# Row loads turned on TensorE, one-operation piece transposes, a fifth summed step and a new instruction list in an H3 convolution and gMLP kernel

## The chip, the cores and the metric

The kernel runs on one core of a Trainium2 chip. A core has five engines that each run their own instruction stream and wait for each other through semaphores: TensorE (PE, matrix products, with the weight loads PEld beside them), VectorE (DVE), ScalarE (ACT), GpSimd (POOL) and SyncE (SP), which here only issues DMAs. The metric is device time in microseconds, lower is better. The kernel before takes 325.17 us (median of 9 runs, 324.26 to 326.95).

## The reference

The input is a sequence `A_q` of 2048 rows and 640 columns. A small vector `c` makes six modulation vectors from one weight, and two blocks follow, each with a layer norm in front and a gated residual behind:

```
sa, ca, ga, sb, cb, gb = silu(c) @ w_mod              # six vectors of 640
h  = layernorm(x) * (1 + ca) + sa
x  = x + ga * A(h, k, v)
h  = layernorm(x) * (1 + cb) + sb
x  = x + gb * B(h)

A: kv = shiftconv4(k, shift_k) * v                    # 4 taps along the sequence, per column
   y  = irfft(rfft(pad(kv)) * rfft(pad(ssm_k)))[:2048] + kv * ssm_D
   return h * y                                       # a long convolution, per column
B: z  = gelu(h @ w_in)                                # 640 -> 2 x 864
   z1, z2 = first half, layernorm(second half)
   return (z1 * (w_sp @ z2 + b_sp)) @ w_out           # w_sp mixes the 2048 rows
```

## The kernel before, in words

Block A works on five units of 128 columns. The long convolution is done as a Fourier transform by matrix products. For each unit there are two inputs, the filter (`XK`, with `ssm_D` added at its first sample, `add_D`, L390) and the product kv (`XU`). `stage1` (L400) multiplies them with a small table, `forward` (L427) with the table M2, in eight steps per unit. ACT keeps the filter's spectrum (`k_item`), and `u_item` (L446) multiplies it with the other one on DVE (`product`, four partial products). The inverse step comes in two forms. In a summed step the partial products are kept in float32 (tile `Tf`, two buffers), two half sums (`csum`, L466) on GpSimd or DVE make `W`, and TensorE does six matmuls. In an unsummed step TensorE takes all four partial products (tile `T`) with twelve matmuls and sums in PSUM. `SUMS` (L35) makes steps 1, 3, 5 and 7 summed ones. The result `Z` is turned, by DMA for units 0 to 3 (`last_stage`, tile `ZT`), on TensorE for unit 4 (`last_stage_pe`), and the last small product (`y`, `yl`) gives y, which is multiplied with the gated norm `gh` (`ym`, `yml`) and added to x (`resid`). `gh_mod` (L644) applies the modulation to `gh`, in products of 512 elements per partition on GpSimd or DVE (`ghm`).

The input kv comes first: k and v are read with transposing DMAs (`load_kv`, L502), four shifted products with diagonal matrices give the taps (`short_conv`, L519, with the diagonals from `sk`), DVE multiplies with v (L543), the result is written to a scratch tensor in DRAM (`kv_scr`) and read back in the layout of the transform.

Three small vectors are loaded at the start or early: `ssm_D` into every 16th partition of `D_col` (L736, after GpSimd has zeroed that tile, L269), `shift_k` into `sk_bf` (L737) and `c` into `c_bf` (L733), in each case with single values or groups of four spread over the partitions.

Block B begins with `z_group` (L838) for groups of four row blocks. The first group is turned on TensorE: it goes in two pieces of two row blocks, and `flip_piece` (L815) makes for each of the five column blocks one TensorE operation of two transposes into a PSUM tile with tag `sm` (two buffers) and one modulation on ACT or DVE. The other groups are turned by DMA. Then TensorE multiplies with `w_in` (tags `pu` and `pz`, two buffers each) and ACT applies gelu. After it the mixing loop (`mix`, `project`, L939 to L971) runs over the 16 row blocks.

All work up to the mixing loop is not run in the order in which it is written. Each piece is registered with `op(...)`, with the engines on which it may run, its inputs and outputs. `ORDER` (L40) is a list written out by hand that names every piece with its number and the engine (P, A, D, G, S) that runs it; `Plan.run` (L112) emits the pieces in this order. So each engine's order, and the order in SP's and ACT's DMA queues, is that of the list. Within it `fill` pieces (L910, sizes in `FILLS`, L34) are matmuls whose result nobody uses.

Of the kernel before, what the change touches and what calls it, by code (L numbers as in the profile page):

```python
# [33 lines left out]
FILLS = (4, 1, 4, )  # L34
SUMS = (1, 3, 5, 7)  # L35
# [5 lines left out]
A76 S3 D6 D94 D7 D12 D11 S4 A1 A9 D8 G95 D96 D115 S13 D103 D10 D116 A117 A118 D80 D5 P1019 P1020 P139 P142 A141 A140  # L41
A144 D17 P20 D97 S77 D98 A100 D143 P18 D81 D104 A105 P148 D109 A99 A106 D110 A111 S14 A112 P145 A150 S15 D21 D19 S16
P24 A26 D121 G101 D102 G119 D107 G108 S507 D120 G113 D25 P22 D23 P130 D511 D131 D132 A147 S28 A146 A149 P163 P153 A164
A154 G114 P136 A137 P151 A152 P127 G30 D128 G129 P159 A160 S82 D84 P155 A156 P219 P133 A134 G42 D512 D513 G135 P157
D514 S27 P161 A162 A158 A220 P35 S29 S78 D36 S79 P31 P167 D169 A168 P170 A171 S40 P33 D172 D32 P173 D34 A510 P176 D178
A174 P37 A175 A177 P165 D38 A166 P193 D194 P221 A222 P179 D180 S508 P45 A515 S39 P203 G195 G196 P223 P189 A224 G66
P181 D204 G205 G206 D190 A516 P209 D210 P225 S0 A2 P197 A198 D517 G138 A182 P213 D214 G215 A226 P47 S41 P183 D184 S83
D46 A518 P191 A192 P207 P199 D200 D48 D526 D527 P229 P243 A230 A244 P49 D50 S549 P239 A208 A240 P245 A246 P227 S509
D522 A228 P43 D44 D185 P233 G124 G125 A234 S85 D87 D519 S88 P249 A250 G186 D523 P237 A238 P231 A232 P550 P247 A248
G216 P217 D218 P241 A242 P235 A236 P291 A292 P255 D256 P552 A553 D524 P211 D212 S51 P251 D90 D252 S554 P293 A528 A294  # L50
G520 P187 P275 D276 A188 G257 G258 G277 P201 A551 A202 P297 A298 P281 D282 P253 A254 G278 P265 D266 P295 P261 A529
A296 D525 P259 D530 P279 A280 A260 P557 D558 P555 S86 P315 A316 P299 D521 D262 G267 G54 G268 S52 S53 A300 S559 A122
S583 P283 G531 A284 D533 D537 D538 S64 D539 P309 A310 D534 D535 D536 G654 P317 A318 P263 P57 P285 D532 A541 P319 A320
P305 A306 D556 G575 D58 D286 G287 D542 A543 D264 D545 P59 P269 P311 A312 P301 A546 D544 D579 A302 D60 P560 D547 D658
D561 P303 A304 D123 D548 P321 P55 A322 G581 G582 P307 A308 D288 P313 A314 D56 D580 P61 D62 P323 D324 P363 P562 G576
A540 G577 G578 G639 P333 A364 P289 D563 A270 P365 A366 P337 A290 D334 P325 P357 D338 P367 D358 P584 D585 A326 P271
D272 A368 P71 S65 D72 P369 A370 G339 G340 P586 D587 P347 D348 P341 A342 P273 A274 P375 A376 D596 P588 D589 G660 S63
S89 G359 P387 A388 G360 D597 G349 G350 P361 D362 P371 A372 P373 A374 D656 P389 G602 A390 P590 D591 P353 D354 P69 D70
P385 P391 D600 A392 A386 A564 P327 D328 D598 S91 G697 D93 P335 A336 D593 P351 G601 P383 A384 P343 P393 D635 G636 P67
A352 D344 D599 A394 P73 P377 P395 A378 D68 P435 A436 P355 A356 P399 D74 G691 D396 D603 P439 A440 D400 P425 G633 S604  # L60
P605 D606 P345 A346 D426 P441 A442 G329 G330 P607 D608 G637 G638 P381 A382 P331 P379 G401 G402 G640 A380 D695 G696
P609 D610 A332 P405 D406 S75 P437 A438 P415 P611 D612 G613 P397 D416 A126 P419 D420 S92 P459 A460 P427 A428 P453 A454
P465 A466 P565 P457 P429 G661 S641 D592 D615 D618 D616 D614 A398 G421 G422 A458 D430 G628 P461 P417 D418 A567 P443
P409 D410 A462 A566 D619 A444 P403 A404 P463 A464 G634 P642 D643 G659 P449 A450 P423 P447 A448 D622 G431 G432 D620
A424 P644 D645 P481 D482 P433 P467 D468 P407 A434 A408 S738 P451 A452 G411 G412 G483 G484 P646 D647 G657 P413 G623
P501 D502 P648 P491 P469 G655 A414 A470 P487 D492 G493 D488 G494 P568 P455 A456 D621 A569 P485 P445 D649 A486 G503
G504 P497 D498 A446 P489 A490 P471 D472 G693 P495 P477 D478 A496 P505 A506 P499 A500 G651 S662 P663 D664 P479 A480
S570 P665 D666 G473 G474 G698 P475 A476 D617 P667 D668 P705 G692 P703 A704 D706 P669 D670 P701 G650 D671 D672 P699
D700 A702 G676 D677 D673 P571 D674 A572 P707 P730 G653 D708 D709 D711 D710 D740 D739 D712 P723 D713 D714 P573 A574
P716 D724 G741 D742 S737 D743 A744 P1021 P745 D731 D746 D755 P747 A748 D675 D715 D756 P749 A750 P753 A754 P751 D752  # L70
D694 D717 P799 A800 D718 D679 P805 A806 P778 G757 P771 D758 D760 A759 P761 A779 A762 P765 D721 A766 D678 D720 A772
D722 D680 D824 D719 D821 D822 P774 P769 P781 A770 P763 D823 D595 A775 P767 A768 D631 D594 D625 D764 A782 G825 D826
D827 D830 A828 D829 S831 D725 D626 P803 D727 A804 D728 P813 A814 D726 D652 D681 D685 D684 P801 A802 P792 P795 A793
D773 D732 D736 A796 P785 D683 P809 A810 D889 D627 P811 P788 A786 A833 D682 D632 D835 D836 A832 A812 D834 D686 D690
D687 D733 D624 D688 D689 P807 A808 A789 P879 A880 P837 A838 P869 P877 A878 D888 D629 A870 P875 D729 D890 D887 A876
P854 G891 D892 D893 A896 D776 D777 D894 D895 A855 D856 D735 P844 A845 D846 P840 D794 A841 D842 P851 P847 A848 P865
A866 D955 A852 D953 D787 P871 D853 A872 D630 D849 D857 P861 A862 P858 S897 A901 D902 A898 P867 D734 D954 A859 D900
P873 A874 A868 D956 G957 D899 P937 P903 A904 A938 P924 P913 D797 D958 A959 A914 D798 D962 P920 D780 A921 D961 D960
D790 S963 A925 D915 P935 A936 D783 D784 P927 A928 D791 G815 D816 P910 A911 D912 D916 P939 A940 A819 D818 P941 A942
D965 P917 P931 D850 A966 D905 P906 A932 A918 D964 D967 D968 P986 P969 A907 A970 D860 D863 D864 D839 D843 A987 P1009  # L80
A1010 D988 P972 G881 D882 A973 P993 A994 D886 P945 A946 D908 D919 P976 D929 D926 D930 A977 D883 P983 D922 D820 A984
D909 D971 D923 D995 D978 D974 P990 D975 A991 D992 P1003 A1004 G947 D948 D949 A884 A817 D985 P933 A934 D885 P979 A980
P1005 A1006 P1001 A1002 P999 A1000 P1011 A1012 D981 D982 P1007 D996 D989 G1013 A950 D1014 D1016 D1018 P997 D1017 A998
D1015 A952 A1008 P943 A944 D951
# [39 lines left out]
def kernel(  # L124
# [37 lines left out]
    d_fft = A_ssm_D.rearrange("(c g) -> g c", g=8)  # L162
# [42 lines left out]
    with ExitStack() as actx:  # L205
# [9 lines left out]
        sk_bf = consta.tile([P, ND, 4], BF16)  # L215
        c_bf = consta.tile([P, ND], BF16)
# [25 lines left out]
        def copy(e, dst, src):  # L242
            (e.copy if e is nc.scalar else e.tensor_copy)(dst, src)  # L243
# [25 lines left out]
        nc.gpsimd.memset(D_col[:], 0.0)  # L269
# [176 lines left out]
        def u_item(u, st):  # L446
# [4 lines left out]

            summed = st in SUMS
            ttag = "Tf" if summed else "T"

            def product(e):
                T_ = new(T, ttag, [P, KP, 2, 2, DU], F32 if summed else BF16)
                e.tensor_tensor(T_[:], tl[pu][:, :, :, None, :].to_broadcast([P, KP, 2, 2, DU]),  # L457
                                tl[KH][:, :, None, :, :].to_broadcast([P, KP, 2, 2, DU]), op=ALU.mult)
            op("D", "prod", product, r=[pu, KH], w=[T], new=[(T, ttag)])
# [99 lines left out]
        def ln1(n):  # L559
# [24 lines left out]
            op("DA", "ln1", stats, r=xs, w=[("mv1", n), ("gh", (0, n // TB))], new=[(tile_, "st1")])  # L584
# [111 lines left out]
        def last_stage_pe(u):  # L696
# [19 lines left out]
            for g in range(NT // TB):  # L716
# [9 lines left out]
                for ns in pieces(g):  # L726
# [3 lines left out]
                    resid(u, g, ns)  # L730


        op("SA", "ldc", lambda e: e.dma_start(c_bf[:], c[0].rearrange("(t p) -> p t", p=P)), w=["c"])  # L733
        op("A", "silut", lambda e: e.activation(warm[:], warm[:], ACT.Silu), w=["silut"])
        op("A", "silu", lambda e: e.activation(sc[:], c_bf[:], ACT.Silu), r=["c", "silut"], w=["silu"])
        op("S", "ldD", lambda e: e.dma_start(D_col[0:P:16, :], d_fft), w=["D"])  # L736
        op("SA", "ldsk", lambda e: e.dma_start(sk_bf[:], A_shift_k.rearrange("(t p) j -> p t j", p=P)), w=["skb"])  # L737
        op("D", "skc", lambda e: e.tensor_copy(sk[:], sk_bf[:]), r=["skb"], w=["sk"])
        index_bits(0, 2)
        f1_table()  # L740
        index_bits(2, 6)
        identity()
        for dt in range(ND):
            load_kv(dt)
            short_conv(dt)
        for u in range(NU):
            d0, du = u * DU, DU
            load_X("XK%d" % u, ssm_fft, u)
            load_X("XU%d" % u, kv_fft, u, [("kvs", (u, h)) for h in range(2 if u == 0 else 1)])
            add_D(u)  # L750
        m2_base()
        for i in range(NKC // KCH):
            m2_chunk(i)
        e_table()
# [265 lines left out]
```

## Time and profile before

| what | value |
|---|---|
| median of 9 runs | 325.17 us |
| the profiled execution, its own time | 327.34 us |
| its span, first to last instruction | 325.5 us |
| PE busy, share | 310.4 us, 95% |
| DVE busy, share | 210.0 us, 65% |
| ACT busy, share | 148.1 us, 45% |
| POOL busy, share | 93.5 us, 29% |
| mean granted TensorE clock | 0.983 |
| first stage of X1U0 starts at | 26.08 us |
| first output step of unit 3 starts at | 122.77 us |
| first MLP matmul starts at | 137.19 us |
| mixing loop starts at | 197.69 us |

How to read it: a profile line gives an engine, the line of the code (often that of a helper, L240 for nearly all matmuls, so the tile names tell more), the operation, output tile and input tiles without buffer numbers, and the shapes. The span is cut into 40 equal slices; a digit is the busy share of an engine in tenths, and PEclk is the clock that TensorE was granted, in tenths of full speed. DVE, for instance, is at 9 of 10 in most slices up to 130 us and at 2 to 4 in the mixing loop. The shares of the whole span are an average over stages with different limits. Every duration comes from one profiled execution.

### The profile page before, as it was taken

Reading aid. Unit: us, or ns where it says so; the run is one execution under the profiler, and the core shown is the slowest. Engines: PE = TensorE matmul, PEld = TensorE weight load, DVE = VectorE, ACT = ScalarE, POOL = GpSimd, SP = SyncE. Lnnn points to the kernel's source line nnn. Section 1 sums busy time; section 2 is a strip of 40 time slices with the busy share of each in tenths; the row PEclk is TensorE's granted clock in tenths of the full one; section 3 lists DMA queues with packets and bytes.
Section 4 is the critical chain, followed back from the end, with each engine's and each line's share of the span. In section 5 each row is a group of like instructions: output and inputs, shape, how many; then the busy total and the mean of one; then the engine's idle time right before and its main releaser. Section 6 shows DMA issues by size and latency. Waiting matters only on the chain.

```text
span 325.5 us, 6384 instructions
## 1 busy us (share of the span) xinstructions
PE 310.4 (95%) x2581; PEld 207.0 (64%) x2589; DVE 210.0 (65%) x464; ACT 148.1 (45%) x255; POOL 93.5 (29%) x121
## 2 busy tenths in 40 slices
PE   5969999899999998899999999999999999999996
PEld 2556889778889896555555555555555555555554
DVE  8967999999999898789675773442332222223333
ACT  4747999897879755377668674000000000000001
POOL 2531724659799898210111120000000000000000
PEclk9979999999999999789999999999999999999999
DMA  6999998997687785004226990465665554422231
GB/s 126 205 258 278 217 293 208 226 244 187 116 236 145 243 179 192 2 1 81 41 42 107 185 250 3 94 132 104 144 137 120 135 114 114 113 50 48 48 50 60
DMA packets 128868, 44.99 MB, mean 138 GB/s; under 512 B 117992, under 2 KB 128072, under 8 KB 128840
## 3 DMA queue, kind: packets, MB, share of 16 engines
q1 hardware_dynamic: 125672, 41.74, 59.2%
q10 hardware_dynamic: 3168, 2.86, 2.7%
q8 instruction: 20, 0.33, 0.4%
q14 instruction: 8, 0.07, 0.1%
HBM read 16.11 MB, written 5.24 MB: 66 GB/s over the span
## 4 chain that ended last, share of the span: by engine, by line
PE 74%; DVE 10%; DMA 7%; SPq 4%; ACT 2%; issue 1%; POOL 0%; DVEq 0%; POOLq 0%; ACTq 0%
PE ps L944 29%; PE pu L240 15%; PE pz L240 13%; PE po L965 9%; DMA ZT<-Z 5%; PE sm L240 5%; SPq L511 3%; PE s L240 3%; DVE T L457 2%; DVE Tf L457 2%; DMA X<-in_A_ssm_k_dram 2%; DVE st L570 1%; DVE big L543 1%; DVE X L243 1%; ACT X L243 1%
## 5 line engine op out<-in xcount | busy, mean ns | idle before, releaser
L944 PE MATMUL ps<-X,wT 128*128 128x432 bf16 x512 | 95.7, 346 | 0.0
L944 PEld LDWEIGHTS <-wT 128*128 128x128 bf16 x512 | 50.1, 98 | 42.2
L957 ACT COPY uT<-pt 128x896 bf16<-128x896 bf16 x1 | 0.9, 906 | 119.1 <-PE pt L956 119.1
L240 PEld LDWEIGHTS <-Z 128*128 128x128 bf16 x320 | 31.7, 100 | 27.5 <-issue 1.6
L240 PE MATMUL pu<-X,M 128*128 128x128 bf16 (+1 forms) x480 | 46.9, 239 | 1.5 <-DVE T L457 0.9
L240 PEld LDWEIGHTS <-M 128*128 128x128 bf16 x480 | 37.7, 99 | 6.9 <-issue 1.6
L947 DVE SCALAR_TENSOR_TENSOR u<-ps,bcol,G 128x432 bf16<-128x432 f32 x18 | 12.0, 668 | 42.1 <-PE ps L944 42.1
L243 ACT CAST X<-s 128x1024 bf16<-128x1024 f32 x32 | 32.7, 1021 | 4.4 <-PE s L240 4.3
L240 PE MATMUL pu<-big,Z 128*128 128x432 bf16 x160 | 33.6, 353 | 0.0
L965 PE MATMUL po<-w_o,uT 128*128 128x320 bf16 (+2 forms) x231 | 33.2, 295 | 0.1
L240 PE MATMUL pz<-big,Z 128*128 128x432 bf16 x160 | 33.2, 351 | 0.0
L466 POOL TENSOR_TENSOR W<-Tf 128x256 bf16<-128x256 f32 x38 | 28.0, 756 | 15.6 <-DVE Tf L457 14.8
L947 DVE SCALAR_TENSOR_TENSOR u<-ps,bcol,M 128x432 bf16<-128x432 f32 x14 | 9.3, 667 | 30.2 <-PE ps L944 30.2
L965 PEld LDWEIGHTS <-uT 128*128 128x128 bf16 (+1 forms) x231 | 22.2, 98 | 9.9 <-issue 0.2
L240 PEld LDWEIGHTS <-G 128*128 128x128 bf16 x360 | 26.9, 98 | 1.8
L243 ACT CAST KH<-pu 128x512 bf16<-128x512 f32 x40 | 22.9, 595 | 6.7 <-PE pu L240 6.7
L457 DVE TENSOR_TENSOR Tf<-pu,KH 128x1024 f32<-128x1024 f32 x20 | 24.2, 1218 | 1.6 <-PE pu L240 1.1
L457 DVE TENSOR_TENSOR T<-pu,KH 128x1024 bf16<-128x1024 f32 x20 | 24.2, 1217 | 0.6 <-PE pu L240 0.5
L967 DVE TENSOR_TENSOR ot<-po,xt 128x320 bf16<-128x320 f32 (+1 forms) x33 | 15.9, 482 | 12.7 <-PE po L965 12.7
L243 ACT CAST Z<-pz 128x512 bf16<-128x512 f32 x35 | 20.3, 590 | 6.7 <-PE pz L240 6.5
L240 PEld LDWEIGHTS <-X 128*128 128x128 bf16 x288 | 18.2, 99 | 7.8 <-DVE X L396 4.6
L888 DVE BATCH_NORM_STATS2 stz<-X 128x6 f32<-128x432 bf16 x32 | 18.2, 591 | 7.1 <-ACT X L882 7.1
(143 smaller groups left out, 413.2 us busy)
## 6 DMA issues: line engine op xcount, KB each, us to landing
wm<-in_w_mod_dram SPq DMA_DIRECT2D x4, 800.0 KB, 6.1
out_dram<-ot SPq DMA_DIRECT2D x15, 160.0 KB, 2.4
big<-in_B_w_in_dram SPq DMA_DIRECT2D x2, 1080.0 KB, 8.3
X<-in_A_ssm_k_dram SPq DMA_DIRECT2D x4, 512.0 KB, 6.2
kv_scr<-big SPq DMA_DIRECT2D x4, 512.0 KB, 3.5
X<-kv_scr SPq DMA_DIRECT2D x4, 512.0 KB, 4.9
xt<-in_A_q_dram SPq DMA_DIRECT2D x3, 640.0 KB, 6.2
wm<-in_w_mod_dram ACTq DMA_DIRECT2D x2, 800.0 KB, 7.3
```

Source lines behind the costliest of these rows:

```text
L240: nc.tensor.matmul(o, lhsT=w, rhs=x, start=start, stop=stop)
L243: (e.copy if e is nc.scalar else e.tensor_copy)(dst, src)
L457: e.tensor_tensor(T_[:], tl[pu][:, :, :, None, :].to_broadcast([P, KP, 2, 2, DU]), tl[KH][:, :, None, :, :].to_broadcast([P, KP, 2, 2, DU] ...
L466: e.tensor_tensor(tl[W][:, :, o, :], T_[:, :, 0, o, :], T_[:, :, 1, 1 - o, :], op=ALU.add if o else ALU.subtract)
L511: e.dma_start_transpose(tl[name][:, o + h * m:o + (h + 1) * m], src[0, h * m:(h + 1) * m, dt * P:(dt + 1) * P])
L543: e.tensor_tensor(vsl, tl[ps][:], vsl, op=ALU.mult)
L570: e.bn_stats(out=st[:, a, :], in_=xt[:, n, a * HS:(a + 1) * HS])
L888: op("D", "stz", lambda e, i=i, n=n, fc=fc: e.bn_stats(out=stz[:, n, fc, :], in_=tl[z2][:, i, fc * FC:(fc + 1) * FC]), r=[(z2, (i, fc))], ...
L944: nc.tensor.matmul(ps[:, :FC], lhsT=wTs[t][:, s_, :], rhs=tl["z2_%d" % (s_ // TB)][:, s_ % TB, fc * FC:(fc + 1) * FC], start=(s_ == 0), st ...
L947: nc.vector.scalar_tensor_tensor(u[:, sl], ps[:, :FC], bcol[:, t:t + 1], z1[t][:, sl], op0=ALU.add, op1=ALU.mult)
L965: nc.tensor.matmul(ps[:, :hi - lo], lhsT=uTs[t][:fsz[ft], ft, :], rhs=w_o[:fsz[ft], ft, lo:hi], start=(ft == 0), stop=(ft == NFT - 1))
L967: nc.vector.tensor_tensor(ot[:, lo:hi], ps[:, :hi - lo], xt[:, t, lo:hi], op=ALU.add)
```

## The change

- The three small vectors are read as rows (`small_load`): `shift_k` as 5 rows of 128 x 4, `ssm_D` as 80 rows of 8, `c` as 5 rows of 128. DVE or GpSimd spreads the 80 x 8 values into a zeroed tile of 80 x 128 (`dwide`). TensorE turns each with small matmuls against the identity (`small_turn`), and DVE or ACT copies the result out of PSUM.
- `MODE` replaces `SUMS`: steps 0, 2, 4, 5 and 7 are summed, five of eight. (A third mode is written in the code and not used.)
- `flip_piece` makes one TensorE operation of all ten transposes of a piece, into one PSUM tile with tag `s1` (one buffer); the five modulations follow.
- Row statistics (`ln1`) are bound to an engine by row block.
- `FILLS` has five entries (17 matmuls) instead of three (9). In the new list ten of them stand in front of the first transform and seven ahead of the first piece's transposes.
- `ORDER` is new throughout: other orders on every engine, other choices of engine. Half sums on GpSimd 38 to 43 and on DVE 2 to 7; row statistics on ACT 5 to 8 and on DVE 11 to 8; `ghm` on GpSimd 27 to 29; residuals on GpSimd 7 to 9; the loads of w_mod and q that stood on ACT's queue are on SP's; the first diagonal is made on ACT; the early gelu of the table load (L758) stands at the end of the list.

The numbers of the pieces shift, so the two lists can't be compared line by line; the list is cut here.

```diff
-FILLS = (4, 1, 4, )
-SUMS = (1, 3, 5, 7)
+FILLS = (4, 5, 1, 4, 3, )
+MODE = ('susussus', 'susussus', 'susussus', 'susussus', 'susussus')
 ORDER = """
-A76 S3 D6 D94 D7 D12 D11 S4 A1 A9 D8 G95 D96 D115 S13 D103 D10 D116 A117 A118 D80 D5 P1019 P1020 P139 P142 A141 A140
...
+D0 D100 D13 D14 A1 D15 G5 A2 A82 G101 D102 D103 S19 S21 D115 D116 A4 A16 D17 D6 D104 P1027 P7 A10 A23 P1028 P8 S83 A11
...
-            summed = st in SUMS
-            ttag = "Tf" if summed else "T"
+            mode = MODE[u][st]
+            summed = mode == "s"
...
-            op("DA", "ln1", stats, r=xs, w=[("mv1", n), ("gh", (0, n // TB))], new=[(tile_, "st1")])
+            op("D" if n % 8 < 4 else "DA" if n % 8 == 4 else "A", "ln1", stats, r=xs, w=[("mv1", n), ("gh", (0, n // TB))], new=[(tile_, "st1")])
...
-        nc.gpsimd.memset(D_col[:], 0.0)
...
-        op("SA", "ldc", lambda e: e.dma_start(c_bf[:], c[0].rearrange("(t p) -> p t", p=P)), w=["c"])
+        def small_load(name, shape, src):
+            op("SA", "ld1", lambda e: e.dma_start(new(name, "KH", shape)[:], src), w=[name], new=[(name, "KH")])
+
+        def small_turn(name, r, fn):
+            def turn(e):
+                fn(new(name, "sm", [P, 512], F32))
+            op("P", "turn1", turn, r=r + ["ident"], w=[name], new=[(name, "sm")])
+        small_load("skr", [ND, P, 4], A_shift_k.rearrange("(t p) j -> t p j", p=P))
+        small_load("Dr", [D // 8, 8], A_ssm_D.rearrange("(c g) -> c g", g=8))
+        small_load("cr", [ND, P], c[0].rearrange("(t p) -> t p", p=P))
...
-        op("S", "ldD", lambda e: e.dma_start(D_col[0:P:16, :], d_fft), w=["D"])
-        op("SA", "ldsk", lambda e: e.dma_start(sk_bf[:], A_shift_k.rearrange("(t p) j -> p t j", p=P)), w=["skb"])
-        op("D", "skc", lambda e: e.tensor_copy(sk[:], sk_bf[:]), r=["skb"], w=["sk"])
+        op("G", "dzero", lambda e: e.memset(new("Dw", "KH", [D // 8, P])[:], 0.0), w=["Dw"], new=[("Dw", "KH")])
+        op("DG", "dwide", lambda e: e.tensor_copy(tl["Dw"][:, 0:P:16], tl["Dr"][:]), r=["Dr"], w=["Dw"])
+        small_turn("tsk", ["skr"], lambda p_: [mm(p_[:, j * ND:(j + 1) * ND], tl["skr"][:, :, j], ident[0:ND, 0:ND], True, True)
+                                               for j in range(4)])
+        small_turn("tD", ["Dw"], lambda p_: mm(p_[:, 0:D // 8], tl["Dw"][:], ident[0:D // 8, 0:D // 8], True, True))
+        small_turn("tc", ["cr"], lambda p_: mm(p_[:, 0:ND], tl["cr"][:], ident[0:ND, 0:ND], True, True))
...
+            def flips(e):
+                p_ = new(pt, "s1", [P, ND, k, P])
+                for dt in range(ND):
+                    for i in range(k):
+                        e.transpose(p_[:, dt, i, :], tl[xn2][:, i0 + i, dt * P:(dt + 1) * P], ident[:])
+            op("P", "hfl", flips, r=["ident"] + [(xn2, i0 + i) for i in range(k)], w=[pt], new=[(pt, "s1")], n=ND * k)
             for dt in range(ND):
-                def flips(e, dt=dt, pt=pt):
-                    p_ = new(pt, "sm", [P, k, P])
-                    for i in range(k):
-                        e.transpose(p_[:, i, :], tl[xn2][:, i0 + i, dt * P:(dt + 1) * P], ident[:])
```

## The prediction

> **What bounds the kernel now.** I read the slices of the span first, then the chain in order of time, then TensorE's timeline.
>
> ```profile
> PE   5969999899999998899999999999999999999996
> POOL 2531724659799898210111120000000000000000
> PEclk9979999999999999789999999999999999999999
> ```
>
> A slice is 8.1 us. TensorE is the spine: nearly full from slice 4 on, with weak places only at the start and around slice 17; the granted clock dips in the same two places. From 137.19 us (first MLP matmul) to the end, TensorE does the same work in both kernels: 188.3 us. So only 137.19 us are in play. I split them at three events of TensorE's timeline: first stage of the first convolution input X1U0 at 26.08, first output step of unit 3 at 122.77, first MLP matmul at 137.19.
>
> The head, from the chain:
>
> ```profile
> 1.94 0.26 SPq L736
> 2.25 0.72 SPq L737
> 3.03 1.68 SPq L511
> ...
> 15.19 5.54 DMA X<-in_A_ssm_k_dram
> 21.04 1.04 PE s L240 x4
> ```
>
> Columns: start, length, what. SP's queue carries the chain from 1.94 to 15.19: the two small loads (L736, L737), then transposing loads one behind another. TensorE idles 2.45 us before 21.04.
>
> The middle, TensorE's timeline:
>
> ```profile
> 35.61 0.60 PE L240 MATMUL pz<-W,G 128*128 128x256 bf16 x6
> 36.05 0.60 PE L240 MATMUL pu<-X,M 128*128 128x256 bf16 x6
> ...
> 37.80 1.05 PE L240 MATMUL pz<-T,G 128*128 128x256 bf16 x12
> 38.69 0.60 PE L240 MATMUL pz<-W,G 128*128 128x256 bf16 x6
> ```
>
> Start to start, a summed inverse step (six matmuls, from W) holds TensorE 0.44 us, an unsummed one (twelve, from T) 0.89. A forward step also costs 0.44, a first-stage group 0.44. Summing the whole list between 26.08 and 122.77 in this way gives 93.0 us of work in 96.7 us: 3.7 us lost.
>
> The joint before the MLP, in the chain, then the clock in stretches (busy us of PE, PEld, DVE, ACT, POOL, then PEclk, DMA share, GB/s):
>
> ```profile
> 133.58 1.70 PE s L240 x4
> ...
> 137.39 1.80 PE pu L240 x5
> 139.19 1.53 PE pz L240 x5
> ```
> ```profile
> 21.00:24.00 3.00, 2.96 (x22) 2.54 (x22) 2.85 (x9) 1.01 (x1) 0.00 (x0) 0.50 1.15 249
> 132.00:135.00 3.00, 3.00 (x41) 1.78 (x42) 2.12 (x6) 1.35 (x2) 0.78 (x1) 0.75 0.02 5
> 135.00:138.00 3.00, 2.43 (x14) 1.44 (x13) 1.83 (x7) 1.59 (x3) 0.90 (x2) 0.50 0.00 0
> ```
>
> [...] the fill of four (L914) runs at half clock, and so do the first ten MLP matmuls: 1.80 and 1.53 us for five, which later take 0.91. That is 1.5 us lost beyond the start at 137.19.
>
> **Head: taken as 1.0 us gained.** The three small loads become rows. SP no longer issues D and the taps (0.81 + 0.72 us) nor waits until 1.38 for D_col's zeroing; its first transposing load can issue near 0.75 instead of 3.03, so everything behind it in SP's queue moves up by as much as 2.3 us. In return ACT issues two more DMAs ahead of its table load (0.42 each by its X load, 0.8 in all), DVE widens D (nearest row, skc: 0.18), GpSimd zeroes a wider tile, TensorE turns two small tiles (tens of ns each), ACT copies both (about 0.2 each) and builds the first diagonal in four pieces, about 0.9 by the slope of its 256- and 512-wide rows (0.43 and 0.53 start to start). The shift taps can go by DVE or ACT, not SP. None of these has a row of its own. Walking DVE's new order from 1.2 us with its own durations gives D's add at 6.3 and the last product with v at 14.1, against 5.95 and 14.8 now (end). ACT, which in the new list does five sines before the first copy, issues the second write to kv_scr near 15.2 (15.90 now). Written and read back as now (5.5 + 4.5 us), X1U0 can start at about 25.4. That is 0.7 by the compute chain, 2.3 by the queue; nothing gained, or 0.8 lost, if ACT's added issues land on the path. I take 1.0, nearer to the compute chain because both writes need all of DVE's products. The ten head fills (five now) run from about 1.6 us, ahead of the first real matmul near 6; they occupy waiting time.
>
> **Middle: 3.4 us less work, 1.3 us more waiting.** Five units each sum five steps instead of four: 5 x 0.44 = 2.2 us off TensorE. The new list also puts two first-stage groups and a forward step ahead of X1U0, into the head's waits: 3 x 0.44 = 1.3. A small turn for c adds 0.1. The sum over the new list is 89.6 against 93.0: 3.4 us.
>
> DVE's list in this stretch falls too, from 92.1 to 88.3 us: five more half sums (0.36 each) and two copies come, but three row statistics (1.04 each), two normalizations and a gate product go to ACT and GpSimd, ACT 83.5 to 84.2, GpSimd 64.5 to 69.3. So nothing but GpSimd gets tighter. What is late next:
> - Unit 3's transposed tile ZT. After its last inverse step come a copy, an issue and 8.53 us of DMA: 9.4 us. Work that covers it: 8.7 us now (0.68 idle), 7.9 in the new list. Cost 0.8.
> - GpSimd, in the stretch where TensorE's list goes from 64 to 104 us. Its demand was 36.7 us for TensorE's 40.0 (the measured row is below, 33.65 busy in 40) and becomes 40.3 for 40.2.
>
> ```profile
> 64.00:104.00 40.00, 39.78 (x502) 34.32 (x504) 38.96 (x62) 33.62 (x48) 33.65 (x34) 1.00 0.79 181
> ```
>
> A half sum there waits behind gate products and residuals of 1.12 us each, and the inverse step waits for the sum, the next product for the buffer (Tf has two). GpSimd has slack before 64 us to run ahead: bounds 0 and 3, taken 0.5, nearer to now, when 9.9 of 10 us busy (90 to 100 us) cost TensorE nothing.
>
> SP now also takes three loads that ACT issued (q row block, two of w_mod). A w_mod load that waits for its single buffer holds back the transposing loads, both w_in loads and ZT behind it; in the new list they stand in the order of their use, and SP stood idle for long stretches after 78 us. Taken as zero, up to 1 us if the cover fails.
>
> **Joint: 1.5 us gained.** From 122.77: now 14.42 to the first MLP matmul plus 1.5 of half clock, 15.9. In the new list the same chain (last inverse step, copy, turns, output steps, statistics, rstd, norm) walked with the same durations brings the normalized rows to 11.0 instead of 11.4, since first-piece statistics come sooner. All ten transposes of a piece are then one TensorE operation with one 5-fold tile: 0.6 at full clock, 1.1 at half. It no longer waits twice for a modulate to free one of two buffers (0.29 and 0.24 idle), but all five modulates begin only after it: three on DVE (0.35 each), two on ACT (0.5). First MLP matmul near 13.95; an output step of 0.8 fills TensorE meanwhile. The fills go from four to seven and start at about 9.1, directly behind a dense product. If they bring the clock up, the MLP starts at full speed: 2.0 gained. If not, seven cost 3.0 us at the 0.43 of the half clock, and 15.5 or more results: 0.4 gained, or a small loss. I take 1.5, nearer to the good end, as the 3.3 us of continuous work after 21.04 sufficed to bring the clock back.
>
> **MLP: 0.3 us lost.** The early table load for gelu is gone from the middle (its position is now the list's end), so the load should come at the first gelu, behind two norms of 0.9 on ACT.
>
> ```profile
> 99.91 1.28 ACT L758 ACT_TABLE_LOAD   x1
> 101.20 0.20 ACT L758 ACTIVATE warm<-warm 128x1 f32<-128x1 f32 x1
> ```
>
> By this row it costs 1.28. [...] TensorE has four accumulators ahead of it (3.6 us of matmuls); by the row, the first gelu ends 3.75 us after the first matmul, just in time[...], taken 0.3. The last norms of the list end about 7.3 us after the last z2 matmul, needed at 7.7: zero, up to 0.5.
>
> **Sum.** -1.0 - 3.4 + 1.3 - 1.5 + 0.3 = -4.3. On the profiled execution: span 325.5 to 321.2, its own time 327.34 (1.84 around the span) to 323.0. That run is 2.2 above the median 325.17; the saving carried to the median gives **320.9**.
>
> **Rivals.**
> - *All covers hold*: head 2.3, joint 2.0, GpSimd and table free: -2.3 - 3.4 + 0.8 - 2.0 = -6.9, 318.3. For: SP carries the head's chain. Against: DVE's products.
> - *The fills don't do what they are for*: clock still halved at the MLP, joint +0.1 instead of -1.5: 322.5. For: the four of now ran wholly at half clock.
> - *A half gain*: GpSimd waits at its bound, 3 instead of 0.5, and the head gives nothing: -4.3 + 2.5 + 1.0 = -0.8, 324.4.
> - *Slower: GpSimd becomes the bound.* A pair of half sums took 1.42 us at 77.66 and 1.71 at 82.20. If its 12 pairs in the 64-to-104 stretch all take 1.71, it needs 43.8 us for TensorE's 40.2: 3.6 of waiting, and the gate products and residuals pushed back stand before rstd of the first piece, 2 x 1.12 = 2.2 more. -4.3 - 0.5 + 3.6 + 2.2 = +1.0, 326.2. It decides from 4.8 us of added waits on.
>
> **Numbers.** Forecast 320.9 (319 to 322): 0.50; all covers 318.3: 0.17; no warm clock 322.5: 0.15; half gain 324.4: 0.08; slower 326.2: 0.10. About 0.3% (1 us) is what a measurement of this kernel can tell from no change; 324.4 lies within it. So faster 0.82, same 0.08, slower 0.10. The range 317.2 to 325.4 leaves out the slower rival and the fastest tail.
>
> **What would show it.** Right: X1U0's first stage near 25, unit 3's output near 119.7, idle TensorE before it 1 to 2 us, first MLP matmul near 133.6 with 0.91 for five from the start. Wrong: TensorE waiting for W or Tf between 64 and 105 us; PEclk 0.5 behind the second fills; a wait for ACT's first gelu.

## The result, and the profile after

The changed kernel takes 323.38 us (median of 16 runs, 322.85 to 324.73) against 325.14 for before (51 runs): a ratio of 0.9947, 95% interval 0.9932 to 0.9962. The forecast was 320.9, by 4.3 us saved on the profiled execution; the medians gain 1.8. The first profiled execution (own time 322.85, span 321.1, clock 1.000) is the fastest of its sixteen.

The slices of the page, rows as in the forecast's fence:

```profile
PE   7898899999998998789999999999999999999996
...
POOL 2366634778999987710010230000000000000000
PEclk9999999999999999999999999999999999999999
```

TensorE is busier in the first and third slice, GpSimd starts earlier (slices 3 and 4), and both dips of the clock are gone. The head, in the chain of work:

```profile
12.52 0.97 ACT X L240 x2
13.53 0.62 PE pu L237 x6
14.17 0.52 ACT KH L240 x2
14.69 3.58 DMA kv_scr<-big
18.32 4.01 DMA X<-kv_scr
```

Compute carries the head now, not SP's queue, and the write to kv_scr took 3.58 us where before took 5.5: X1U0's first stage came at 22.38 instead of 26.08. The middle, by TensorE's waits from 22 to 124 us (waited for, us in total, times, longest), after:

```profile
PE pu L237 <- DVE Tf L454: 1.4, 3, 0.5
PE sm L237 <- DMA ZT<-Z: 0.8, 1, 0.8
PE s L237 <- DVE X L240: 0.5, 1, 0.5
PE pu L237 <- DVE T L454: 0.5, 1, 0.5
```

Three of the four are waits for VectorE, and none is for GpSimd's half sums. The wait for ZT stands at 104.37, at unit 2's output; unit 3's output, where the forecast put 0.8 us, waits for nothing. The joint, in the timelines of TensorE, VectorE and ScalarE; in brackets the idle time ahead of a row and who ended it:

```profile
129.69 0.72 PE L841 MATMUL s<-ident,Z 128*128 128x128 bf16 x10
131.05 0.34 PE L237 MATMUL pz<-big,Z 128*128 128x432 bf16 x1
132.93 0.90 PE L237 MATMUL pz<-big,Z 128*128 128x432 bf16 x4 [1.54 <-DVE Z L853]
...
139.90 1.27 PE L237 MATMUL pu<-big,Z 128*128 128x432 bf16 x6 [0.95 <-DVE Z L853]
```
```profile
130.51 0.73 DVE L853 TENSOR_SCALAR Z<-s,cb_col,sb_col 128x256 bf16<-128x256 bf16 x2 [0.33 <-issue]
132.46 0.41 DVE L853 TENSOR_SCALAR Z<-s,cb_col,sb_col 128x256 bf16<-128x256 bf16 x1 [1.23 <-ACT Z L851]
```
```profile
131.41 1.02 ACT L851 ACTIVATE Z<-s,sb_col,cb_col 128x256 bf16<-128x256 bf16 x2 [1.90 <-DVE Z L853]
```

The five modulates run two, two, one: each engine waits for the other. The forecast had them side by side.

Since the first profiles lie near opposite ends of their kernels' runs (327.34 and 322.85), both kernels were profiled again. The new pair (own times 326.27 and 323.93, each some 0.6 above its median) gives the balance:

| stretch | before | changed | difference | forecast |
|---|---|---|---|---|
| start to X1U0's first stage | 26.45 | 22.86 | -3.6 | -1.0 |
| to unit 3's first output step | 96.67 | 95.86 | -0.8 | -2.1 |
| to the mixing part (joint and MLP) | 73.47 | 75.31 | +1.8 | -1.2 |
| to the end of the span | 127.7 | 128.1 | +0.4 | 0 |
| span | 324.3 | 322.1 | -2.2 | -4.3 |

The head gave more than forecast. The joint, forecast as a gain, is a loss in this pair, where both executions have half-clock time in it. The first pair, with about twice as much of it there before and none after, gives -3.7, -0.8, -0.2 and +0.4, together -4.4.

### The profile page after: what moved, and what is told of

It is laid out like the page before. It is cut to its first block, busy times and chain, and to the rows that moved or that the text cites. A ratio compares the mean times of both kernels' runs of the same rounds, so it can differ in the third digit from the quotient of the medians.

```text
span 321.1 us, 6384 instructions
## 1 busy us (share of the span) xinstructions
PE 306.6 (95%) x2566; PEld 203.4 (63%) x2573; DVE 210.4 (66%) x450; ACT 154.8 (48%) x275; POOL 104.0 (32%) x130
## 4 chain that ended last, share of the span: by engine, by line
PE 72%; DVE 9%; DMA 7%; ACT 6%; POOL 2%; issue 2%; POOLq 0%; SPq 0%; DVEq 0%; ACTq 0%
PE ps L964 28%; PE pu L237 14%; PE pz L237 13%; PE po L985 9%; PE sm L237 4%; DVE Tf L454 3%; PE s L237 3%; DMA ZT<-Z 3%; DMA X<-in_A_ssm_k_dram 2%; ACT X L240 1%; DMA X<-kv_scr 1%; POOL gh L651 1%; DMA kv_scr<-big 1%; ACT M L340 1%; DVE X L240 1%
## 5 line engine op out<-in xcount | busy, mean ns | idle before, releaser
L964 PE MATMUL ps<-X,wT 128*128 128x432 bf16 x512 | 95.9, 346 | 0.2 <-ACT X L923 0.2
L237 PEld LDWEIGHTS <-Z 128*128 128x128 bf16 x320 | 31.0, 98 | 29.9 <-DVE Z L853 3.2
L237 PE MATMUL pu<-X,M 128*128 128x128 bf16 (+1 forms) x480 | 45.4, 237 | 2.7 <-DVE Tf L454 1.4
L468 POOL TENSOR_TENSOR W<-Tf 128x256 bf16<-128x256 f32 x43 | 32.9, 781 | 16.2 <-DVE Tf L454 15.5
L237 PE MATMUL pu<-big,Z 128*128 128x432 bf16 x160 | 32.8, 346 | 0.9 <-DVE Z L853 0.9
L240 ACT CAST X<-s 128x1024 bf16<-128x1024 f32 x30 | 30.6, 1021 | 2.9 <-PE s L237 2.9
L454 DVE TENSOR_TENSOR Tf<-pu,KH 128x1024 f32<-128x1024 f32 x25 | 30.2, 1217 | 1.4 <-ACT KH L240 0.6
L237 PEld LDWEIGHTS <-G 128*128 128x128 bf16 x330 | 25.2, 98 | 2.5
L237 PE MATMUL sm<-big,dg 128*128 128x512 bf16 (+3 forms) x73 | 19.7, 379 | 0.7 <-DVE big L545 0.3
L237 PE MATMUL s<-F1bd,X 128*128 128x256 bf16 x128 | 19.2, 272 | 0.7 <-DVE X L240 0.5
```

Source lines behind the costliest of these rows:

```text
L237: nc.tensor.matmul(o, lhsT=w, rhs=x, start=start, stop=stop)
L454: e.tensor_tensor(T_[:], (tl[pu] if src is None else tl[src])[:, :, :, None, :].to_broadcast(shape), tl[KH][:, :, None, :, :].to_broadcast ...
L468: e.tensor_tensor(tl[W][:, :, o, :], T_[:, :, 0, o, :], T_[:, :, 1, 1 - o, :], op=ALU.add if o else ALU.subtract)
L964: nc.tensor.matmul(ps[:, :FC], lhsT=wTs[t][:, s_, :], rhs=tl["z2_%d" % (s_ // TB)][:, s_ % TB, fc * FC:(fc + 1) * FC], start=(s_ == 0), st ...
```

## Experiments

Below, "the changed kernel" is 323.38 (ratios 0.9947 and, in its second series, 0.9927). All ratios are to before on the same chip. The chips of the experiments differ (before's median was 324.94 to 325.64 on them), and the changed kernel ran again only on the chip of the old loads, the row statistics and the gate products. So a difference to 323.38 of less than about 0.7 us says little. Where a trace can say more, stretches are counted within it: from X1U0's first stage to unit 3's first output step the changed kernel takes 95.86 us, from there to the mixing part 74.71 at full clock.

**Before, again** (no edit).

> The kernel before, unchanged, to learn how its own executions spread. Theory A (the profiled execution of before carried half-clock time that its typical execution doesn't have): most executions show a mean granted clock above 0.99 and lie near 325; those near 0.98 lie about 2 us above; in a new profile the stretch before the first MLP matmul has more clock than the 0.50 to 0.75 of the first. Rival B (every execution of before has the halved clock, and the changed kernel lost the gain elsewhere): 0.98 to 0.985 in nearly all executions, no relation of clock to time, and the new profile again shows 0.5 near 21 to 24 and 133 to 140 us. In both the median is 325.1 and the ratio 1.000.

325.64, ratio 0.9999 (0.9983 to 1.0015). The clock of an execution takes a few values: of 66 executions here, 4 lie at 0.999 to 1.000 (mean 324.8 us), 51 at 0.993 to 0.995 (325.4), 10 at 0.988 or 0.989 (326.4), 1 at 0.983 (327.8). So neither reading as stated holds, but A's mechanism does: half-clock time comes in portions of about 0.0055 of the span, each costs 0.7 to 1.4 us, and a typical execution has one. The new profile has two, in these stretches (busy us of PE, PEld, DVE, ACT, POOL, then PEclk):

```profile
20.00:24.00 4.00, 2.58 (x19) 2.21 (x20) 2.79 (x9) 0.65 (x1) 0.92 (x1) 0.65 1.16 236
...
131.00:134.00 3.00, 2.69 (x78) 2.30 (x75) 2.90 (x12) 0.79 (x2) 1.00 (x2) 0.97 0.00 0
134.00:137.00 3.00, 2.67 (x12) 1.35 (x11) 1.57 (x6) 1.34 (x3) 0.00 (x0) 0.50 0.03 5
137.00:140.00 3.00, 2.76 (x17) 1.30 (x15) 2.43 (x8) 1.67 (x4) 0.90 (x2) 0.96 0.00 0
```

From the missing clock of the last three rows, taken as time at half clock (0.50 at 134 to 137), one portion is 2 x (0.09 + 1.5 + 0.12) = 3.4 us long. The forecast's profile (0.983) had three: in the same way 3.4 us between 20 and 25 us (clock 0.66 on average) and 6.8 between 132 and 141 (0.62).

**The changed kernel, again** (no edit).

> The changed kernel, unchanged, for a second profile (its first was the fastest of its 16 executions) and as the mark for the three runs beside it. Theory (its executions rarely meet a half-clock window, those of before usually meet one or two): median 323.4, ratio 0.995, granted clock 0.993 to 1.000; first stage of X1U0 near 22.6, first output step of unit 3 between 118.2 and 120.2. Rival (the first profile showed the usual execution): 118.2 again, and then the median should have been 322.9.

323.38, ratio 0.9927 (0.9905 to 0.9949); X1U0 at 22.86, unit 3 at 118.72. Of its 22 executions in both series 16 lie at 0.998 to 1.000. A typical execution has lost its half-clock portion; by the means above this is worth 0.7 us or so of the 1.8. The second profile is one of the six that have one, in the joint:

```profile
130.00:133.00 3.00, 1.82 (x44) 1.49 (x43) 1.44 (x7) 1.02 (x2) 2.45 (x4) 1.00 0.03 5
133.00:136.00 3.00, 2.59 (x9) 1.19 (x10) 2.93 (x9) 2.20 (x3) 3.00 (x3) 0.65 0.00 0
136.00:139.00 3.00, 3.00 (x22) 1.66 (x20) 1.88 (x9) 2.48 (x5) 2.14 (x4) 0.78 0.00 0
```

**Two PSUM tiles for the transposes of a piece.**

```diff
-p_ = new(pt, "s1", [P, ND, k, P])
+new(pt, "s1", [P, ND, k, P]); new(pa, "sm", [P, 4, k, P])   # pa: ScalarE's column blocks
```

> The changed kernel with one thing altered: the ten transposes of a piece go into two PSUM tiles, one read by VectorE's scalings, one by ScalarE's (and one copy of the last modulation row is moved forward into ScalarE's idle time to free the second tile). Theory (VectorE's and ScalarE's scalings wait for each other because they read one PSUM tile): both engines start together, the first MLP matmuls' wait falls from 1.54 us to about 0.5 and the second piece's from 0.95 to below 0.3, total 1.5 to 2 us below the changed kernel, about 321.6. Rival (the scalings are ordered by something else, or TensorE would wait for normalization anyway): waits unchanged, 323.0 to 323.6.

322.14, ratio 0.9885 (0.9857 to 0.9913): about 1.2 us below the changed kernel, somewhat less than expected, and faster than both kernels. (The edit also moves one copy of ScalarE forward, to free the second tile.) The waits went as the theory said:

```profile
131.47 1.05 DVE L855 TENSOR_SCALAR Z<-s,cb_col,sb_col 128x256 bf16<-128x256 bf16 x3 [0.33 <-issue]
```
```profile
131.35 1.02 ACT L853 ACTIVATE Z<-sm,sb_col,cb_col 128x256 bf16<-128x256 bf16 x2 [0.57 <-ACT gb_bf L644]
```
```profile
132.58 0.90 PE L237 MATMUL pz<-big,Z 128*128 128x432 bf16 x4 [0.22 <-DVE Z L855]
```

Both engines start within 0.12 us of each other and TensorE waits 0.22 instead of 1.54; the 0.95 of the second piece is gone. From unit 3's output to the mixing part it is 72.95 us, 1.8 less than the changed kernel's first profile (74.71), both at full clock. All six executions stay at 0.999 or 1.000, and so, at 0.998 or above, do the fifteen of the two later runs with two tiles, against 16 of 22 of the changed kernel: with the pause shorter, the half clock was not met. Two tiles are enough; why the engines took turns at one tile, the run does not tell.

**Without the last two fills.**

```diff
-FILLS = (4, 5, 1, 4, 3, )
+FILLS = (4, 5, 1, )
```

> The changed kernel without its last two fills (seven matmuls ahead of the transposes of the first piece). Theory (the fills keep the clock up): TensorE at half clock from the transposes on, the transposes 1.1 us instead of 0.57 and the first ten MLP matmuls 1.5 us longer, total about 1.5 us above the changed kernel, 324.9. Rival (the clock is up anyway since TensorE's pauses got short): granted clock still 1.00 there, total the same to 0.5 us lower, 322.9 to 323.4.

325.51, ratio 0.9985 (0.9963 to 1.0008): 2.1 us above by the medians. The half clock is back, in 12 of 14 executions for about two portions or more (0.989 and below). Stretches of its profile:

```profile
132.00:135.00 3.00, 1.93 (x40) 1.49 (x38) 1.12 (x4) 1.02 (x2) 2.92 (x4) 0.50 0.00 0
135.00:138.00 3.00, 2.76 (x8) 1.19 (x9) 2.93 (x7) 1.62 (x2) 3.00 (x4) 0.50 0.03 5
```

The transposes took 1.25 us by their row instead of 0.72. The fills do what the forecast took them to do: they keep the clock up (with them 16 of 22 executions lie at 0.998 or above, without the last two none of 14). How much of the 2.1 us is theirs is less sure. In this profile the joint is 1.1 us longer, and the middle, which the edit leaves alone, 1.5: a piece of v came late, VectorE waited 0.79 us for it at 60 us.

**Small vectors loaded as before** (D and the taps in columns at the head of SP's queue, GpSimd's zeroing, no small turns).

> The changed kernel with the small vectors loaded as before (D and taps in columns at the head of SP's queue, GpSimd's zeroing of D's column, no small turns on TensorE); the rest of the list is kept. Theory (the head's gain of 3.7 us is real but VectorE, full from 28 us on, gives most of it back): X1U0's first stage near 25.5, the whole 0.5 to 1.5 us above the changed kernel, about 324.4. Rival (the head's gain is carried to the end): X1U0 near 25.5 and the whole 2.5 to 3.5 us above, 326 to 327. Second rival (the head's gain is due to the new order of the list, not to the rows): X1U0 within 0.7 us of 22.6, the whole unchanged.

325.41, ratio 1.0005 (0.9988 to 1.0022), 2.0 us above. X1U0 came at 24.33, 1.5 us later than in the second profile of the changed kernel and 1.95 later than in the first. From there on the trace is that of the first one, both at full clock: 95.95 and 74.68 us for the middle and the joint with the MLP, against 95.85 and 74.71; the span is 1.7 longer. So what the rows give at the head is carried to the end, as the first rival had it, though with less at the head than its 25.5; VectorE does not take it back. Without the rows the rest of the change gained nothing in the median, in a list that was written for them. The other 2 us or so of the head's gain belong to the new order by subtraction; no run tests that. The clock stays at 1.00 from 14 to 24 us here (a step of six matmuls takes 0.60 us throughout): the first dip went with the new list, not with the rows.

**Four sums per unit instead of five.**

```diff
-MODE = ('susussus', 'susussus', 'susussus', 'susussus', 'susussus')
+MODE = ('susuusus', 'susuusus', 'susuusus', 'susuusus', 'susuusus')
```

> The changed kernel with four summed inverse steps per unit instead of five: step 4 is left unsummed, its ten half sums are left out, the rest of the list is kept. Theory of the forecast (TensorE's work sets the time of the middle, a summed step saves 0.44 us): 5 times 0.44 = 2.2 us above the changed kernel, 325.6. Rival (VectorE is as full as TensorE there, so half of the saving is waited away): 0.5 to 1.2 us above, 323.9 to 324.6. Second rival (the half sums cost as much as they save): within 0.3 us of 323.4.

327.71, ratio 1.0052 (1.0030 to 1.0074): 4.3 above, twice the forecast's term and outside every theory. Counted from X1U0 to unit 3's output it is 100.15 us, also 4.3 more. Of this, 2.2 is TensorE's work; the rest appears as waits, above all for products (the longest 1.36 us at 92 us). The list was written for five sums, so this is not the price of a sum in a list written for four; it speaks against the reading that the sums gained nothing.

**VectorE's row statistics over fewer columns.**

```diff
-in_=xt[:, n, a * HS:(a + 1) * HS]
+in_=xt[:, n, a * HS:a * HS + 64]
```

> The changed kernel with VectorE's row statistics of the first normalization taken over 64 columns of each half instead of 320; this leaves out part of the statistics. TensorE's work is unchanged, VectorE's falls by some 11 times 0.35 = 3.8 us between X1U0 and unit 3's output. Theory (VectorE bounds the middle together with TensorE): 1.5 to 3.5 us below the changed kernel, 320 to 322. Rival (TensorE's work sets the middle, as the forecast had it): 0 to 0.5 us below.

324.03, ratio 0.9943 (0.9920 to 0.9966): no gain. The edit took less than expected out of the middle, 2.6 us of VectorE (91.4 to 88.7): only four of its eight row statistics lie there, at 40 to 47 us; the other four come before X1U0. From 42 us on TensorE in the changed kernel is busy 10.00 of 10 us, and VectorE with its shorter statistics stood 1.87 us waiting for it at 47. So VectorE does not set the pace in this stretch, and the theory falls for the middle as a whole; of the stretches around it the run says nothing.

**GpSimd's gate products over half of their columns.**

```diff
+w = du // 2 if e is nc.gpsimd else du
```

> The changed kernel with GpSimd's gate products taken over half of their columns; this leaves out the modulation of the other half. TensorE's and VectorE's instructions are unchanged, GpSimd is some 14 us less busy. Theory (VectorE's operations from SBUF to SBUF run longer while GpSimd works, some 3 us in the middle): VectorE's norm, gate and residual operations return from 0.51, 0.49 and 0.57 us toward 0.44, 0.42 and 0.42, VectorE's busy time between X1U0 and unit 3's output falls by 1 to 2 us, the whole 1 to 3 us below the changed kernel. Rival (GpSimd matters only through the half sums that wait behind it): the durations stay, TensorE's waits for sums fall, the whole 0 to 1 us below.

322.55, ratio 0.9902 (0.9880 to 0.9923): 0.8 below by the medians, where both readings overlap. VectorE's durations speak for the theory: between X1U0 and unit 3's output its busy time fell by 1.1 us (91.4 to 90.3), its gate products (scale part) went from 0.49 to 0.42 on average, its residual adds from 0.57 to 0.43, its norms only from 0.51 to 0.49. First the changed kernel (its first profile), then this one, VectorE's timeline:

```profile
66.06 0.42 DVE L651 TENSOR_TENSOR gh<-gh,gca_bf 128x512 bf16<-128x512 bf16 x1
...
69.77 0.97 DVE L651 TENSOR_TENSOR gh<-gh,gca_bf 128x512 bf16<-128x512 bf16 x1
```
```profile
65.78 0.42 DVE L651 TENSOR_TENSOR gh<-gh,gca_bf 128x512 bf16<-128x512 bf16 x1
...
69.45 0.49 DVE L651 TENSOR_TENSOR gh<-gh,gca_bf 128x512 bf16<-128x512 bf16 x1
```

The same product takes 0.42 us alone and 0.97 beside GpSimd's two full ones, 0.49 beside two of half width. The norm before it stays long in both (0.93 at 68.51, 0.94 at 68.18), beside a half sum that the edit leaves as it was. All four rows, two products and two norms, end a fixed time behind an instruction of GpSimd: the products 0.29 us behind GpSimd's product (which ends at 70.45 and 69.65), the norms 0.19 and 0.18 behind the half sum (69.25 and 68.94). So in these rows VectorE seems to stand until GpSimd's instruction has ended, and a shorter one lets it go sooner (the product by 0.48 us).

**1.3 us of empty TensorE work at three places.**

```diff
-FILLS = (4, 5, 1, 4, 3, )
+FILLS = (4, 5, 1, 4, 3, 2, 2, 2, )   # at 34 to 37, 42 to 49, or 69 to 73 us
```

> The changed kernel with three fills of two matmuls each (1.3 us of TensorE work that computes nothing) put between unit 0's forward steps, 32 to 37 us. Theory (behind X1U0 VectorE's eight products of 1.13 us each, one behind another, set the pace until 40 us, so TensorE work there costs nothing, and taking it away, as the change does, saved nothing): 0 to 0.4 us above the changed kernel, 323.4 to 323.8. Rival (TensorE's work counts wherever it stands, as the forecast summed it): 1.3 us above, 324.7.

> The same three fills put where TensorE is full, 42 to 48 us. Theory (there TensorE sets the pace): 0.9 to 1.5 us above the changed kernel, 324.3 to 324.9. Rival (loads landing near 62 us, or VectorE, set the pace through this stretch too): 0 to 0.4 us above.

> The changed kernel with the three fills of two matmuls (1.3 us of TensorE work) put at 69 to 73 us, where VectorE never rests between 63 and 80 us and runs longer beside GpSimd. Theory (VectorE sets the pace there): 0 to 0.5 us above the changed kernel, 323.4 to 323.9; the later first stages less than 0.4 us late. Rival (TensorE's work counts there as it does at 42 to 48 us): 1.3 to 1.9 us above.

At 34 to 37 us: 324.40, ratio 0.9969 (0.9952 to 0.9987), 1.0 above the changed kernel, spread from 322.88 to 326.47. In its profile nothing is late by the first stage at 41.5 us (17.5 us after X1U0, as in the changed kernel), and 0.7 by unit 3's output. At 42 to 49: 325.31, ratio 0.9998 (0.9982 to 1.0014), 1.9 above by the medians, 0.9 from X1U0 to unit 3's output. At 69 to 73: 325.47, ratio 1.0015 (0.9999 to 1.0030), 2.1 above, 1.6 by the stretch. So the theory of two stretches paced by VectorE falls for the second; for the first the trace agrees and the total is inconclusive. TensorE work costs about its own length at 42 to 49 and at 69 to 73 us, although TensorE has waits near the second; that an operation put ahead of a forward step also delays the product that follows it is a reading, not tested.

**Two copies exchanged** (X1U1's first copy to ScalarE, its third to VectorE).

> The changed kernel with two copies exchanged: the first copy of X1U1 (39.1 us, 1.13 us of VectorE, TensorE waits for it 0.53 us) goes to ScalarE, the third (45.9 us) to VectorE, where TensorE is full. Work of every engine is the same to 0.2 us. Theory (VectorE's work counts between 27 and 40 us and not between 42 and 58): 0.4 to 1.0 us below the changed kernel, 322.4 to 323.0. Rival (where VectorE's work stands doesn't matter): within 0.3 us of 323.4.

326.00, ratio 1.0024 (1.0007 to 1.0040): 2.6 slower, a miss; by the stretch from X1U0 to unit 3's output 2.3. VectorE's queue, then TensorE's:

```profile
47.48 1.23 DVE L240 CAST X<-s 128x1024 bf16<-128x1024 f32 x1 [2.50 <-PE s L237]
```
```profile
50.52 0.61 PE L237 MATMUL s<-F1bd,X 128*128 128x256 bf16 x4 [1.76 <-DVE X L392]
```

The copy put into VectorE's queue stood 2.5 us waiting for TensorE, with the add of D behind it, and TensorE then waited 1.76 for that add. The experiment tested the order of a queue, not the theory.

**Two tiles, the exchange, and the add of D to the third filter piece one product later.**

> Two PSUM tiles for the transposes of a piece, the two copies exchanged, and VectorE's add of D to the third filter piece put one product later (it stood waiting for a load near 62 us ahead of that product). If the three are independent: 1.24 (measured) + 0.4 to 1.0 + 0 to 0.4 below the changed kernel, 320.8 to 321.8. If the later stretches absorb the earlier ones: 322.1, as with two tiles alone.

323.83, ratio 0.9958 (0.9942 to 0.9973), 1.7 above two tiles alone: the exchange spoils it.

**The finish of the statistics later.** VectorE's three small operations at 36.5 us go behind the copy that TensorE waits for; alone, and with two tiles and the later add.

> The changed kernel with VectorE's three small operations that finish the first eight rows' statistics (1.5 us with their stretching, 36.5 to 38 us) moved behind the copy of X1U1 that TensorE waits for; no engine's work changes, and nothing needs them before GpSimd's rstd near 44 us. Theory (VectorE's products set the pace of the stretch behind X1U0): unit 0's last product and that copy 1 to 1.5 us earlier, the whole 0.3 to 1.0 us below the changed kernel, 322.4 to 323.1. Rival (the list is balanced so closely that the next stretch takes it back): within 0.3 us of 323.4.

> The same, with two PSUM tiles for the transposes of a piece and the add of D to the third filter piece one product later. If the gains add: 0.3 to 1.0 us below two tiles alone (322.1), 321.1 to 321.8. If the later stretches take them back: 322.1.

Alone: 324.03, ratio 0.9968 (0.9953 to 0.9984). Counted from X1U0, the first stage behind that copy came 1.2 us sooner (16.3 instead of 17.5), as expected, but at 45.5 us only 0.1 was left, and unit 3's output came after 95.85 us: the rival is right. With two tiles: 321.13 (320.93 to 321.98), ratio 0.9888 (0.9866 to 0.9911), the lowest median of all, but by the ratio no better than two tiles alone. Its trace has 95.07 us from X1U0 to unit 3's output, 0.8 less than the changed kernel; whether the gains add stays open.

## Why the prediction was right and wrong

Right: the direction; that the small loads at the head of SP's queue cost time (2.0 us of the median when they are put back); the fills that keep the clock up (0.998 or above in 16 of 22 executions, in none of 14 without the last two); and the table load: it took 1.28 us at 135.05, the first gelu followed at 136.34, and no wait for a gelu stands among TensorE's waits (the 0.3 us forecast for it was the author's estimate). The size was wrong, in four terms.

**The carried saving.** "That run is 2.2 above the median 325.17; the saving carried to the median gives 320.9." This step failed. The profiled execution held three half-clock portions where a typical one has one, two of them at the joint, and the forecast's sum for the joint counted 1.5 us of half clock there as going away; in most executions part of that is not there to be saved. The half clock was read from this one execution: before's 66 executions show that the number of portions varies, by their mean clocks from none (0.999 to 1.000) to three (0.983). In the forecast's profile the first ran from 20.84 to 24.26 us, so the clock was at half before TensorE's work began at 21.04; that this work brought it back was the author's estimate. The profiled pair did differ by 4.4 us of span, but by luck: the head gave 2.7 more than forecast, the middle 1.3, the joint with the MLP 1.0 and the end 0.4 less. The second pair differs by 2.2, the medians by 1.8.

**The joint's modulates.** The step "three on DVE (0.35 each), two on ACT (0.5)", taken side by side, failed. With one tile for all five each engine waited for the other (VectorE 1.23 us, ScalarE 1.90 at the first piece): 1.54 and 0.95 us of TensorE's wait. Two tiles left 0.22 of these waits and took 1.2 us off the median. The forecast gave the two rotating tiles of before a cost (0.29 and 0.24) and the single tile none. In the second profile the half clock followed the pause: TensorE is busy 1.82 of 3 us from 130 to 133, and the clock then reads 0.65 and 0.78. In the first, with 1.46 of 3 us busy there, the clock stayed at 1.00.

**The head: -1.0 forecast, -3.6 measured.** The mis-sized terms are the write to kv_scr and its read-back, taken as 5.5 + 4.5 us from before and measured as 3.58 + 4.01; besides, ScalarE issued the write at 14.69 and not near 15.2. So even the upper bound of 2.3 by the queue was too low. With the old loads the write was issued at 16.2 and its read-back could start at 20.0, so the shorter write goes with the new list, not with the rows; why it is shorter was not tested.

**The middle: -2.1 forecast, -0.8 measured.** The work fell as forecast: TensorE has 1104 matmuls in this stretch instead of 1146. The waiting was wrong: by the forecast's sum of 89.6 us of work, TensorE lost 6.3 of the 95.9 us, not 5.0. The step that failed is "nothing but GpSimd gets tighter". It rested on sums of VectorE's durations over 97 us: 92.1 falling to 88.3. Measured over this stretch, VectorE's busy time is 92.2 and, in the first profile of the changed kernel, 91.6. Of the 3.3 us between, some 2.5 are instructions that ran longer than before, beside a busier GpSimd (71.3 us in the stretch against 67.8, first profiles): ten norms at 0.51 instead of 0.44, seven gate products at 0.49 instead of 0.42, three residual adds at 0.57 instead of 0.42, three adds of D at 0.52 instead of 0.22 (second profiles). With the half-width gate products the last three groups came back to 0.42, 0.43 and 0.27, the norms only to 0.49. The four rows given with that run ended 0.18 to 0.29 us behind an instruction of GpSimd; for the others this was not shown.

The 1.3 us of work put ahead of X1U0 was counted whole, yet in the stretch behind X1U0 unit 0's eight products (1.13 us each) already followed one another on VectorE in both kernels, with only small operations between: in the 16 us from X1U0 on TensorE was busy 15.39 us before and is busy 14.64 now (second profiles). Work taken away there left a wait. GpSimd's half sums, given 0.5, cost no wait by name. Of the forecast's signs of being wrong one came, a wait of 0.5 us for Tf near 73 us, but for VectorE's product, not for GpSimd.

What stays open: how the middle's missing 1.3 us divides between VectorE's longer instructions, the stretch behind X1U0 and the new order. Removing VectorE work at 40 to 47 us gained nothing, removing GpSimd work gained 0.8, and adding 1.3 us of TensorE work cost 1 to 2. Open too is what the new order gives apart from the rows. In a list this tightly coupled, single terms do not add.

## What to carry to other kernels

Before a saving in one profile is carried to a median, ask whether that execution is typical: half-clock portions of 3.4 us are enough to move it by 2 us (before took 327.8 us in its execution with three, 325.4 on average with one), and a second profile shows it. When several small tiles are merged into one, count the readers: here two engines that read one PSUM tile ran one after the other, and TensorE waited 1.54 and 0.95 us for them. A sum of work over a long stretch says nothing about the short ones, and with fixed in-order queues an operation moved to an engine with slack can cost twice its length by standing at the head of its queue (here a copy of 1.23 us, and 2.6 us of the median).

## What the runs showed of the hardware

The mean clock of an execution falls into steps (1.000, 0.994, 0.989, 0.983), so one number tells how many half-clock portions of 3.4 us it had (0.989 two, 0.983 three, by the two profiles of before). One bf16 product from SBUF to SBUF on VectorE took 0.42 us with GpSimd at rest, 0.97 beside its full products and 0.49 beside half-width ones, and an add of 16 columns 0.93 in the changed kernel and 0.23 with the half-width products. With the same instructions ahead of it, X1U0's first stage came anywhere from 22.4 to 24.2 us in thirteen profiles on several chips, behind the same write and read-back.
